# Score products of two heads on the two halves of TensorE's rows, in an fp32 attention and gated feed-forward kernel

## The chip, the core and the metric

The kernel runs on one core of a Trainium2 chip. The metric is the device time of one execution in microseconds, as the median of several runs. The engines are TensorE (PE; its weight loads PEld), VectorE (DVE), ScalarE (ACT), GpSimd (POOL) and the sync engine (SP), which here issues nearly all loads.

## The reference

```python
# q, k, v: (4 batches, 8 heads, 576, 64) fp32; hidden = 32
scores = scale * np.matmul(q, k.transpose(0, 1, 3, 2))
x = (psi_rel / psi_i)[..., None]          # from positions alone
h = np.maximum(x @ w1 + b1, 0.0)
bias = h @ w2                             # one 576 x 576 bias per head
scores = scores + bias.transpose(2, 0, 1)[None, :, :, :]
scores = scores - np.max(scores, axis=-1, keepdims=True)
attn = np.exp(scores)
attn = attn / (np.sum(attn, axis=-1, keepdims=True) + 1e-09)
return np.matmul(attn, v).astype(np.float32)
...
# attn as (2304 tokens, 512), w_in (512, 2048), w_out (2048, 512)
h = x @ w_in
relu6 = np.clip(h + 3.0, 0.0, 6.0)
g = h * relu6 / 6.0
return (g @ w_out).astype(np.float32)
```

The weights w_in and w_out arrive in 64-bit form and are turned into pairs of fp16 numbers (a high and a low part) on the chip.

## The kernel before, in words

**Units and tiles.** Two heads form a pair, four pairs a batch. The 576 query rows are cut in two units: rows 0 to 255 (`u` = 0) and 256 to 575 (`u` = 1). A tile is 128 query rows of one head; a unit 0 has four tiles, a unit 1 five. All 16 units 0 come first. Tile number `n` runs over all of them; of a pair's unit 0 the tiles are row block 0 of head 0, row block 0 of head 1, row block 1 of head 0, row block 1 of head 1 (`ORDER`).

**Two forms of score products.** Batches 0 and 1 of unit 0 (the first 32 tiles) are *direct* (`direct`): score products, transposes of the weights of attention and their product with v are done in fp32. `load_direct` loads q and k of a pair. Head 0 lies on partitions 0 to 63, head 1 on 64 to 127; q is spread to a tile with zeros in the other head's rows (memset on GpSimd, line 378), so that a product over all 128 rows gives one head's scores. All later tiles split q and k into a high and a low part in a packed 32-bit form and take three products a head on 64 rows each, the two heads in turn (line 549); the last row block of a unit 1 takes three products on 128 rows with a zero-filled tile. One fp32 product is two records in the trace, each with its own weight load; one of line 549 is one record.

**A step.** `front(n)` issues, in this order: the score products of tile n+1 if it is direct (`qk_step`), the softmax maximum of tile n on VectorE (line 561, reads the scores and the bias, writes `bt`), for later tiles the score products here instead, the transposes of tile n-2 (line 620, 128 rows, fp32), loads (`aux`), the product with v once a unit is complete (lines 662, 673, then a multiply on VectorE, line 689). `back(n)` issues the exponential on ScalarE (line 572). Between the steps come pieces of other work at fixed rates: the position bias (lines 847 to 864), the preparation of w_in and w_out (lines 244 to 280 and 138) and the feed-forward network (hidden layer line 779 with lines 756 to 769, output layer line 802).

**PSUM.** Until tile 45 there are three score banks (`s_bank`, two PSUM banks each), which score products, transposes, products with v and bias products share in turn, and two `w_bank`s. From tile 45 on there are two and four.

**What sets the order.** A scheduler takes the program order as a priority and sets each engine's order when the program is built, until tile 45; from there TensorE follows the program order. Each engine then runs its list in order and waits where an input or a buffer isn't there. The loads (lines 377, 380, 433, 483 and 489 for the bias, 175 for v, 244 for w) stand in the sync engine's queue in the same way; `behind()` keeps a load behind the last bias load.

Of the kernel before, what the change touches and what calls it, by code (L numbers as in the profile page):

```python
# [10 lines left out]
F32 = mybir.dt.float32  # L11
# [7 lines left out]
S = 576  # L19
# [3 lines left out]
HALF = S // 2  # L23
# [10 lines left out]
def attention_moe_kernel(  # L34
# [15 lines left out]
    nc = tc.nc  # L50
# [11 lines left out]
    qk_p = ctx.enter_context(tc.tile_pool(name="qk", bufs=4))  # L62
# [17 lines left out]
    def s_bank(name):  # L80
        return pools["ps_s"].tile([128, 2, 512], F32, tag="s", name=name)
# [140 lines left out]
    def dq(c):  # L222
        return nc.scalar if c in cfg["act"] else nc.sync
# [3 lines left out]
    def behind(k=-1):  # L227

        return tc.issue_after(bias_loads[k]) if len(bias_loads) > max(k, 0) else nullcontext()
# [138 lines left out]
    qk_t = {}  # L368
    st_t = {}

    def load_direct(b, p):
        t = qk_p.tile([128, 512 + S], F32, tag="hi", name="qk0")
        q, k = t[:, 0:512].rearrange("p (a b) -> p a b", a=2), t[:, 512:512 + S]
        for s in range(2):
            rows = slice(64 * s, 64 * s + 64)
            with behind():
                dq("q").dma_start(out=q[rows, s], in_=qk[b, p][rows, 0:256])
            nc.gpsimd.memset(q[rows, 1 - s], 0.0)
        with behind():
            dq("q").dma_start(out=k, in_=qk[b, p][:, 256:256 + S])  # L380
        qk_t[b, p, 0] = (t, k)

    QW = (256, 320)
    KC0 = (256, 0)
# [128 lines left out]
    s_t = {}  # L513
# [4 lines left out]
    def qk_step(n):  # L518
        b, p, t = tiles[n]
        i, s = ORDER[t]  # L520
        u = int(t >= 4)
        if direct(b, p, t):
            ps = s_bank("s_ps")
            q, k = qk_t[b, p, 0]
            c = 256 * s + 128 * i
            for a in range(2):
                nc.tensor.matmul(  # L527
                    out=ps[:, a, 0:HALF], lhsT=q[:, c:c + 128], rhs=k[:, a * HALF:(a + 1) * HALF]
                )
            s_t[n] = ps  # L530
            return
        if s:
            return
        if i == 4:
            hi, lo, tz = qk_t.pop((b, p, u))
            every = slice(0, 128)
            parts = [(every, tz[:, 0], tz[:, 1])]
        else:
            hi, lo = qk_t[b, p, u][:2]
            c = QC0[u] + 128 * i - 256 * u  # L540
            qs = slice(c, c + 128)
            parts = [(r, hi[r, qs], lo[r, qs]) for r in (slice(0, 64), slice(64, 128))]
        for k in range(len(parts)):
            s_t[n + k] = s_bank("s_ps")
        for k, (q, m) in enumerate(((0, hi), (0, lo), (1, hi))):
            for a in range(2):
                cs = slice(KC0[u] + a * HALF, KC0[u] + (a + 1) * HALF)
                for j, (rows, *w) in enumerate(parts):
                    nc.tensor.matmul(  # L549
                        out=s_t[n + j][:, a, 0:HALF], lhsT=w[q], rhs=m[rows, cs],  # L550
                        start=(k == 0), stop=(k == 2),
                    )
# [47 lines left out]
    def direct(b, p, t):  # L600
        return b < cfg["fb"] and t < 4
# [329 lines left out]
    def front(n):  # L931
        late = at(n + 1) and not direct(*tiles[n + 1])
        if at(n + 1) and not late:
            qk_step(n + 1)
# [6 lines left out]
        if late:  # L941
            qk_step(n + 1)
# [32 lines left out]
    def aux(n):  # L975
        b, p, t = tiles[n]
        k = unit_no[n]
        l = t - UT[int(t >= 4)][0]
        if l == 0 and PAIRS <= k + 2 < len(units):
            b2, p2, u2 = units[k + 2]  # L980
            if direct(b2, p2, 4 * u2):
                load_direct(b2, p2)
            else:
                load_qk(b2, p2, u2)
        if k + 1 < len(units) and not direct(units[k + 1][0], 0, 4 * units[k + 1][2]):
            if l == 1:
                split_qk_a(*units[k + 1])
            if l == 2:
                split_qk_b(*units[k + 1])
            if l == 3:  # L990
                split_qk_c(*units[k + 1])
        if l == 0 and k < 13:
            load_v(*units[k])
        if l == 1 and 13 <= k + 1 < len(units):
            load_v(*units[k + 1])
        if not direct(b, p, t):
            if l == 2:
                split_v_a(*units[k])
            if l == 3:
                split_v_b(*units[k])  # L1000
        if b + 1 < B and t < 4 and p >= 1:
            if b + 1 not in vgen:
                vgen[b + 1] = v_scale(b + 1)
            next(vgen[b + 1], None)
# [26 lines left out]
    for cs in (slice(512, LT), slice(0, 512)):  # L1031
        nc.vector.tensor_scalar(
            out=T[:, cs], in0=T[:, cs], scalar1=w1_sb, scalar2=None, op0=ALU.mult
# [13 lines left out]
    for c, pat in enumerate(pats):  # L1047
        for k in range(4):
            if pat[k]:
                rows = slice(32 * k, 32 * k + 32)  # L1050
# [95 lines left out]
    for g in range(cfg["g0"]):  # L1146
        bias_next()
        if g == 0:
            steps(gen_w, aw, cfg["rwi"])
        if 0 <= g - cfg["gq"] < PAIRS:  # L1150
            load_direct(0, g - cfg["gq"])
        if g >= 1:
            steps(gen_w, aw, cfg["rw0"])
    for n in range(-1, NT + 7):
# [14 lines left out]
        if done is not None and done != (0, 0):  # L1169
            b, u = done  # L1170
# [71 lines left out]
```

## Time and profile before

| | us |
|---|---|
| median of 3 runs | 714.4 |
| lowest and highest | 710.62, 718.45 |
| the profiled execution | 713.93 |
| its span in the trace | 712.1 |

The span is the stretch from the first to the last instruction in the trace; 1.8 us of the profiled execution lie around it. The median and the profiled execution differ by 0.5 us. The profile has one core, with a mean granted TensorE clock of 0.976 of full speed.

### The profile page before, as it was taken

Reading aid. Unit: us, or ns where it says so; the run is one execution under the profiler, and the core shown is the slowest. Engines: PE = TensorE matmul, PEld = TensorE weight load, DVE = VectorE, ACT = ScalarE, POOL = GpSimd, SP = SyncE. Lnnn points to the kernel's source line nnn. Section 1 sums busy time; section 2 is a strip of 40 time slices with the busy share of each in tenths; the row PEclk is TensorE's granted clock in tenths of the full one; section 3 lists DMA queues with packets and bytes.
Section 4 is the critical chain, followed back from the end, with each engine's and each line's share of the span. In section 5 each row is a group of like instructions: output and inputs, shape, how many; then the busy total and the mean of one; then the engine's idle time right before and its main releaser. Section 6 shows DMA issues by size and latency. Waiting matters only on the chain. (4 is left out here: it accounts for less than half of the span.)

```text
span 712.1 us, 15431 instructions
## 1 busy us (share of the span) xinstructions
PE 657.8 (92%) x5538; PEld 471.2 (66%) x5538; DVE 498.2 (70%) x1263; ACT 491.8 (69%) x994; POOL 257.0 (36%) x350
## 2 busy tenths in 40 slices
PE   6667799898889998999998899999999999999998
PEld 2214566676466676788786788767776777777775
DVE  7999788899777697758866877777767776310310
ACT  6996678788676798758866876888568854631530
POOL 3212021346222154236642563465335611420420
PEclk9889999999999999999999999999999999999999
DMA  8987987856695996999999998969995865000000
GB/s 279 337 284 215 312 241 207 252 151 182 173 216 145 240 224 172 226 245 204 224 222 236 193 205 179 218 158 185 187 199 135 171 144 111 2 10 28 2 11 28
DMA packets 178637, 127.35 MB, mean 179 GB/s; under 512 B 139136, under 2 KB 147584, under 8 KB 178560
## 3 DMA queue, kind: packets, MB, share of 16 engines
q1 hardware_dynamic: 168768, 111.03, 67.0%
q10 hardware_dynamic: 9792, 15.34, 6.9%
q8 instruction: 43, 0.70, 0.4%
q14 instruction: 34, 0.28, 0.1%
HBM read 74.43 MB, written 15.34 MB: 126 GB/s over the span
## 5 line engine op out<-in xcount | busy, mean ns | idle before, releaser
L779 PE MATMUL h_ps<-x,wi 128*128 128x256 f16 (+1 forms) x1536 | 198.6, 287 | 8.0 <-DVE t L762 4.5
L802 PE MATMUL o_ps<-g,wo 128*128 128x256 f16 (+1 forms) x1536 | 196.6, 287 | 0.0
L779 PEld LDWEIGHTS <-wi 128*128 128x128 f16 x1536 | 147.1, 98 | 54.1 <-issue 12.3
L802 PEld LDWEIGHTS <-wo 128*128 128x128 f16 x1536 | 147.1, 98 | 47.0 <-issue 9.9
L758 POOL TENSOR_TENSOR g<-t,g 128x256 f16<-128x256 f32 (+1 forms) x128 | 101.9, 806 | 135.3 <-ACT g L756 134.4
L572 ACT ACTIVATE bt<-bt,sm 128x576 f32<-128x576 f32 x144 | 110.6, 768 | 56.1 <-DVE sm L561 55.3
L138 DVE SCALAR_TENSOR_TENSOR hl<-bt,sm,hl 128x576 f16<-128x576 f32 x112 | 98.7, 891 | 23.8 <-POOL hl L115 13.7
L762 DVE SCALAR_TENSOR_TENSOR t<-t,t,h_ps 128x320 f32<-128x320 f32 (+1 forms) x112 | 56.1, 516 | 68.4 <-ACT t L769 67.5
L115 POOL TENSOR_SCALAR hl<-bt,sm 128x576 f16<-128x576 f32 x56 | 48.9, 873 | 109.4 <-DVE sm L584 55.1
L864 PE MATMUL b_ps<-z,w_sb 128*32 128x288 f32 x576 | 68.5, 445 | 18.6 <-ACT z L851 15.5
L756 ACT ACTIVATE g<-t 128x256 f16<-128x256 f32 (+1 forms) x128 | 55.5, 440 | 35.3 <-DVE t L762 34.5
L404 POOL TENSOR_TENSOR qkl<-st,qkh 128x576 fp32r<-128x576 f32 (+2 forms) x48 | 56.1, 1188 | 43.9 <-ACT qkh L397 42.2
L769 ACT ACTIVATE t<-h_ps,t,hr 128x320 f32<-128x320 f32 (+1 forms) x112 | 64.7, 586 | 9.5 <-PE h_ps L779 6.3
L561 DVE CUSTOM_DVE_ANT_0 bt<-s_ps,bt 128x576 f32<-128x576 f32 x80 | 58.9, 751 | 10.3 <-PE s_ps L549 8.3
L864 PEld LDWEIGHTS b_ps<-z,w_sb 128*32 128x32 f32 x576 | 21.2, 113 | 54.1 <-ACT z L851 30.0
L812 ACT ACTIVATE ot<-o_ps,os 128x256 f32<-128x256 f32 (+1 forms) x32 | 15.9, 497 | 55.7 <-PE o_ps L802 54.7
L847 DVE TENSOR_SCALAR z<-T,nbp 128x576 f32<-128x576 f32 x85 | 51.0, 641 | 3.3 <-PE b_ps L864 3.2
L851 ACT ACTIVATE z<-T,bp 128x576 f32<-128x576 f32 x59 | 45.1, 767 | 11.7 <-PE b_ps L864 8.1
L561 DVE CUSTOM_DVE_ANT_0 bt<-s_ps,k 128x576 f32<-128x576 f32 x64 | 46.2, 752 | 6.3 <-PE s_ps L549 5.0
L527 PE MATMUL s_ps<-qk 128*128 128x288 f32 x128 | 41.2, 448 | 9.9 <-DVE sm L561 4.4
L121 ACT ACTIVATE hl<-bt,sm 128x576 f16<-128x576 f32 x56 | 43.1, 769 | 6.8 <-issue 1.5
L580 DVE TENSOR_SCALAR sm<-sm 128x1 f32<-128x1 f32 x112 | 16.8, 150 | 41.7 <-ACT bt L572 41.4
(118 smaller groups left out, 880.7 us busy)
## 6 DMA issues: line engine op xcount, KB each, us to landing
bt<-bias SPq DMA_DIRECT2D x64, 288.0 KB, 5.5
bias<-bo ACTq DMA_DIRECT2D x36, 288.0 KB, 4.8
w<-in_w_in_dram SPq DMA_DIRECT2D x16, 512.0 KB, 5.5
vs<-in_vp_dram SPq DMA_DIRECT2D x24, 320.0 KB, 5.1
st<-in_qk_dram SPq DMA_DIRECT2D x16, 448.0 KB, 4.4
wo<-in_w_out_dram SPq DMA_DIRECT2D x10, 512.0 KB, 7.1
k<-bias SPq DMA_DIRECT2D x32, 144.0 KB, 3.7
bt<-bias SPq DMA_DIRECT2D x32, 144.0 KB, 3.2
```

Of the source, the lines that this page charges most:

```text
L138: nc.vector.scalar_tensor_tensor(out=out, in0=full, scalar=scale, in1=high, op0=ALU.mult, op1=ALU.subtract)
L404: nc.gpsimd.tensor_sub(out=lo[:, c:c + w], in0=t[:, c:c + w], in1=hi[:, c:c + w].bitcast(F32))
L561: nc.vector.tensor_tensor_reduce(out=halves(bt), in0=ps, in1=halves(src), op0=ALU.add, op1=ALU.min, scale=-0.125, scalar=3.0e38, accum_out ...
L572: nc.scalar.activation(out=bt, in_=bt, func=AF.Exp, scale=-1.0, bias=sm[:, 0:1], accum_out=total)
L756: nc.scalar.activation(out=g[:, 0], in_=uu, func=AF.Copy)
L758: e.tensor_sub(out=g[:, 1], in0=uu, in1=g[:, 0])
L762: nc.vector.scalar_tensor_tensor(out=t_t[f], in0=t_t[f], scalar=cols(f)[2], in1=h_t.pop(f)[:, 0:n], op0=ALU.min, op1=ALU.mult,)
L769: nc.scalar.activation(out=t_t[f], in_=h_t[f][:, 0:n], func=AF.Relu, scale=cols(f)[0], bias=cols(f)[1],)
L779: nc.tensor.matmul(out=h_t[f][:, 0:n], lhsT=wi[:, a, c, f * 128:(f + 1) * 128], rhs=x[:, e, c], start=(k == 0), stop=(k == 3 * KC - 1),)
L802: nc.tensor.matmul(out=ops[:, 0:n], lhsT=wo[:, a, f, e * 128:(e + 1) * 128], rhs=g_t[f][:, r], start=(f == 0 and a == 0 and r == 0), stop= ...
L847: nc.vector.tensor_scalar(out=z, in0=src, scalar1=nbp[:, col], scalar2=None, op0=ALU.max)
L864: nc.tensor.matmul(out=pss[a][32 * k:32 * k + 32, 0:HALF], lhsT=w2_sb, rhs=z[:, a * HALF:(a + 1) * HALF],)
```

## The change

`load_direct` loads q and k of a pair with one transfer into one tile and writes no zeros. `qk_step` does nothing for a tile of head 1; for a tile of head 0 it takes two score banks and issues the products of both heads, each on the 64 rows of its head, the heads in turn for each half of the columns. The later lines move up by four (line 549 becomes 545, 620 becomes 616).

```diff
     def load_direct(b, p):
-        t = qk_p.tile([128, 512 + S], F32, tag="hi", name="qk0")
-        q, k = t[:, 0:512].rearrange("p (a b) -> p a b", a=2), t[:, 512:512 + S]
-        for s in range(2):
-            rows = slice(64 * s, 64 * s + 64)
-            with behind():
-                dq("q").dma_start(out=q[rows, s], in_=qk[b, p][rows, 0:256])
-            nc.gpsimd.memset(q[rows, 1 - s], 0.0)
+        t = qk_p.tile([128, 512 + S], F32, tag="hi", name="qk0")[:, 0:256 + S]
         with behind():
-            dq("q").dma_start(out=k, in_=qk[b, p][:, 256:256 + S])
-        qk_t[b, p, 0] = (t, k)
+            dq("q").dma_start(out=t, in_=qk[b, p][:, 0:256 + S])
+        qk_t[b, p, 0] = t
...
+        if s:
+            return
         if direct(b, p, t):
-            ps = s_bank("s_ps")
-            q, k = qk_t[b, p, 0]
-            c = 256 * s + 128 * i
+            m = qk_t[b, p, 0]
+            for k in range(2):
+                s_t[n + k] = s_bank("s_ps")
             for a in range(2):
-                nc.tensor.matmul(
-                    out=ps[:, a, 0:HALF], lhsT=q[:, c:c + 128], rhs=k[:, a * HALF:(a + 1) * HALF]
-                )
-            s_t[n] = ps
-            return
-        if s:
+                cs = slice(256 + a * HALF, 256 + (a + 1) * HALF)
+                for k in range(2):
+                    r = slice(64 * k, 64 * k + 64)
+                    nc.tensor.matmul(
+                        out=s_t[n + k][:, a, 0:HALF], lhsT=m[r, 128 * i:128 * i + 128], rhs=m[r, cs]
+                    )
             return
```

On TensorE, before, at the end of the first batch and the start of the second (`qk_848` is the fifth pair's tile of q and k, `bt` a tile's attention weights; x2 and x5 are instructions in a row):

```order
L620 MATMUL t_ps<-eye_sb,bt 128x128 x5
L527 MATMUL s_ps<-qk_848 128x288 x2
L620 MATMUL t_ps<-eye_sb,bt 128x128 x5
L662 MATMUL pv_ps<-atf,vf 64x256 x10
L673 MATMUL pv_ps<-eye_sb,r_sb 64x128 x4
L527 MATMUL s_ps<-qk_848 128x288 x2
L620 MATMUL t_ps<-eye_sb,bt 128x128 x5
L527 MATMUL s_ps<-qk_848 128x288 x2
```

The same place on TensorE in the changed program (`qk_832` is the fifth pair's tile there):

```order
L616 MATMUL t_ps<-eye_sb,bt 128x128 x10
L658 MATMUL pv_ps<-atf,vf 64x256 x10
L669 MATMUL pv_ps<-eye_sb,r_sb 64x128 x4
L526 MATMUL s_ps<-qk_832 128x288 x4
L616 MATMUL t_ps<-eye_sb,bt 128x128 x10
```

Products and transposes of one tile in turn have become products of two tiles, then transposes of two tiles.

On VectorE, before, around the last tiles of the fourth pair's second row block (`k_776` is a kept bias tile; the ISA rows are the softmax maximum and its read-out):

```order
L561 ISA bt,sm<-s_ps,k_776 128x576
L561 ISA sm 128x1
L138 SCALAR_TENSOR_TENSOR wo<-cu,w2s,wo 128x512
L144 TENSOR_REDUCE m_v_855<-vparts 128x1
L561 ISA bt,sm<-s_ps,k_776 128x576
L561 ISA sm 128x1
L1103 TENSOR_SCALAR x<-x,r_w1c 128x2x256
L147 TENSOR_SCALAR m_v_855<-m_v_855 128x1
L561 ISA bt,sm<-s_ps,bt 128x576
```

The same place on VectorE in the changed program (`k_763` is that bias tile):

```order
L557 ISA bt,sm<-s_ps,k_763 128x576
L557 ISA sm 128x1
L557 ISA bt,sm<-s_ps,k_763 128x576
L557 ISA sm 128x1
L1099 TENSOR_SCALAR x<-x,r_w1c 128x2x256
L273 TENSOR_SCALAR cu,w2top<-cu 128x512
L144 TENSOR_REDUCE m_v_835<-vparts 128x1
L138 SCALAR_TENSOR_TENSOR wo<-cu,w2s,wo 128x512
L557 ISA bt,sm<-s_ps,bt 128x576
```

The softmax maxima of the two heads now stand one behind the other, and the other work stands between the pairs.

## Rows read from the trace of the kernel before

**Rows 1.** The page: busy time of each engine, share of the span, instructions.

```profile
PE 657.8 (92%) x5538; PEld 471.2 (66%) x5538; DVE 498.2 (70%) x1263; ACT 491.8 (69%) x994; POOL 257.0 (36%) x350
```

**Rows 2.** Stretches: length, then each engine's busy time, granted clock, DMA share, GB/s.

```profile
54.00:100.00 46.00, 34.62 (x195) 23.00 (x187) 38.88 (x113) 31.02 (x60) 7.38 (x14) 0.93 0.87 255
100.00:184.00 84.00, 77.98 (x561) 57.49 (x559) 75.22 (x223) 68.00 (x142) 33.63 (x43) 0.96 0.73 207
184.00:230.00 46.00, 41.82 (x370) 26.29 (x369) 35.73 (x98) 32.22 (x57) 11.66 (x14) 0.96 0.72 168
230.00:712.00 482.00, 467.14 (x4178) 352.89 (x4170) 298.80 (x721) 315.72 (x670) 191.45 (x253) 1.00 0.72 154
```

**Rows 3.** Instructions of lines 527, 549: shortest, median, longest ns, first and last start.

```profile
L527 PE MATMUL s_ps<-qk x128: 405/407/849, 54.7 to 157.3; 128*128 128x288 f32 x128
...
L549 PE MATMUL s_ps<-qkh x192: 285/395/607, 158.2 to 592.1; 64*128 64x288 f32 x192
```

**Rows 4.** Stretches, line 527 alone: length, PE busy, PEld busy, clock, DMA.

```profile
54.00:100.00 46.00, 18.87 (x56) 10.55 (x56) 0.93 0.87 255
100.00:160.00 60.00, 22.33 (x72) 12.76 (x72) 0.97 0.75 212
```

**Rows 5.** Waits of VectorE, 54 to 184 us: total us, times, longest.

```profile
DVE vparts L177 <- DMA va<-in_vp_dram: 7.0, 5, 2.0
...
DVE bt L561 <- PE s_ps L527: 1.5, 1, 1.5
```

**Rows 6.** Waits of TensorE's matmuls, 54 to 184 us.

```profile
PE s_ps L527 <- DVE sm L561: 4.4, 3, 2.5
PE s_ps L527 <- DVE xr L689: 4.1, 2, 3.7
```

**Rows 7.** Timeline of TensorE's matmuls from 102.9 us: start, us, what.

```profile
102.93 1.14 PE L527 MATMUL s_ps<-qk 128*128 128x288 f32 x4
103.91 0.71 PE L620 MATMUL t_ps<-eye_sb,bt 128*128 128x128 f32 x5
```

**Rows 8.** Chain of work that ended last: start, us, what.

```profile
473.05 0.79 PE s_ps L549 x6
...
483.49 0.99 PE s_ps L549 x12
```

**Rows 9.** Timeline of TensorE's matmuls from 204.9 us.

```profile
204.92 1.18 PE L864 MATMUL b_ps<-z,w_sb 128*32 128x288 f32 x16
206.03 4.43 PE L802 MATMUL o_ps<-g,wo 128*128 128x256 f16 x39
```

**Rows 10.** Timeline of TensorE's matmuls from 138.4 us.

```profile
138.37 2.78 PE L779 MATMUL h_ps<-x,wi 128*128 128x256 f16 x24
140.99 1.14 PE L527 MATMUL s_ps<-qk 128*128 128x288 f32 x4
```

**Rows 11.** Timeline of GpSimd from 74.9 us; in brackets the idle time before.

```profile
74.92 0.66 POOL L378 MEMSET qk<- 64x256 f32 x2 [9.53 <-PE s_ps L527]
79.70 0.66 POOL L258 TENSOR_SCALAR wo<-wo 128x512 f32<-128x512 f32 x1 [4.12 <-ACT cu L256]
```

**Rows 12.** The sync queue: line 377 (ns as in rows 3), and its timeline.

```profile
L377 SPq DMA_DIRECT2D qk<-in_qk_dram x16: 471/594/656, 6.4 to 119.1; - x16
...
76.33 1.25 SPq L377 DMA_DIRECT2D qk<-in_qk_dram  x2
```

**Rows 13.** Transfers by line: count, KB each, median us from issue to landing.

```profile
st<-in_qk_dram SPq DMA_DIRECT2D x8, 416.0 KB, 6.0
```

**Rows 14.** Timeline of VectorE, 93 to 103 us.

```profile
93.13 0.34 DVE L1103 TENSOR_SCALAR x<-x,r_w1c 128x512 f16<-128x512 f16 x1
...
95.03 0.76 DVE L561 CUSTOM_DVE_ANT_0 bt<-s_ps,bt 128x576 f32<-128x576 f32 x1 [1.50 <-PE s_ps L527]
...
95.72 0.68 DVE L273 TENSOR_SCALAR_CACHE_REDUCE cu<-cu 128x512 f32<-128x512 f32 x1
...
102.95 0.75 DVE L138 SCALAR_TENSOR_TENSOR wo<-cu,w2s,wo 128x512 f16<-128x512 f32 x1
```

## Prediction, made before the changed kernel had run

> **What bounds the kernel now.** I read the page first: TensorE is busy for 92% of the span, VectorE for 70% and ScalarE for 69% [rows 1]. That is an average over very different stages, so the second view is a table by stretches [rows 2]. After 230 us TensorE is busy for 467.1 of 482 us: there the end moves only with TensorE's work, or with the moment at which that stage starts. The work that the change touches lies ahead of it: the 128 matmul records of line 527 run from 54.7 to 157 us [rows 3], 18.87 us of busy time before 100 us and 22.33 us after it [rows 4]; at four records a tile that is 14 tiles and 18 tiles. So the question is how much sooner the first 230 us end. In 54 to 100 us TensorE is busy for 34.6 of 46 us and VectorE for 38.9; in 100 to 184 us it is TensorE 78.0 of 84, VectorE 75.2; in 184 to 230 us TensorE 41.8 of 46, VectorE 35.7 [rows 2]. Neither engine is alone the bound there. The two wait lists for 54 to 184 us say who waits for whom: VectorE's longest wait is for a load (va, 7.0 us in five waits), and for score products it waited once, for 1.5 us [rows 5]; the matmul side's longest waits on line 527 are for VectorE's softmax, 4.4 us, and for its normalising multiply, 4.1 us [rows 6]. So before 100 us TensorE mostly waits for a VectorE that itself waits for data, and after 100 us TensorE is nearly full.
>
> **The products themselves.** A tile of the old form takes 0.98 us: its four records start at 102.93 us and the transposes behind them at 103.91 us [rows 7]. Two tiles are 1.96 us. No fp32 product of which two take the two halves of the rows in turn is in the trace. The nearest rows are those of line 549: a packed pair of heads, 12 matmuls on 64 rows each, took 0.99 us in the chain, and six matmuls on 128 rows took 0.79 us [rows 8]. Six rounds of two therefore ran abreast, and the pair paid 0.20 us more than its six rounds. That fp32 products run abreast too is shown by another row: 16 fp32 records of the bias products, in four column groups, had passed after 1.11 us (204.92 to 206.03 us) [rows 9], where four unpacked ones need 0.98 us. So a pair of the new form is four rounds of 0.245 us plus 0.20 us, 1.18 us, and saves 0.78 us. With 16 pairs that is **12.5 us of TensorE time**; the bounds are 15.7 us (nothing paid for the change of form) and a loss of 3.2 us (no two abreast, 16 times 0.20 us paid).
>
> The 0.20 us is what the row shows for going from 128 rows to 64 and back. The Trainium skill, "TensorEngine Tiling (Array Packing)", section Key Properties, says that changing the tiling mode drains TensorE; it speaks against this change, since every pair stands between transposes on 128 rows. It gives no price: with no drain the sum would be 15.7 us, with the row's 0.20 us it is 12.5 us, and the trace agrees with the rule.
>
> **What of it reaches the end.** Seven pairs run before 100 us: 7 x 0.78 = 5.5 us at full clock. TensorE has 11.4 idle us there and waits mostly for VectorE, whose waits for va are not TensorE's doing. I take 1.5 us of the 5.5; bounds 0 and 5.5. Nine pairs run after 100 us: 7.0 us, in a stage with 6.0 idle us of TensorE. Here the products are ahead of the hidden-layer matmuls (line 779) that fill the gaps, 0.109 us each (24 of them from 138.37 to 140.99 us) [rows 10]. The order of the changed program shows where they go: 120 of the 192 of the first unit stand ahead of the first line-549 product, 90 before; 30 x 0.109 = 3.3 us of work pulled ahead. VectorE limits it: 8.8 idle us in the stage, some of it waits that stay. I take 5.5 of the 7.0 us; bounds 2 and 7. The sum is **7.0 us**. What is late next is VectorE: at 84 - 5.5 us the stage holds 75.2 us of its work, 96%. The steady stage after 230 us holds the same work as before, so I carry the 7.0 us to the end unchanged.
>
> **The rest of the diff.** The 16 memsets (line 378) go. They cost GpSimd 0.3 us each; the worst of them stood 9.53 us waiting for line 527 to free its buffer, but the operation behind it then waited another 4.12 us for ScalarE, so nothing was lost by it [rows 11]: zero. If that cover were gone, it would be worth at most those 9.53 us to the preparation of w_out, none to the products. The three loads of a pair become one: 16 issues fewer of 0.594 us each, 9.5 us of the sync queue's time [rows 12], which is free where that queue waits for buffers anyway. The new load has the size of an existing one, which landed in 6.0 us [rows 13]. The fifth pair's load was issued at 76.3 us and its first product ran at 102.9 us [rows 7, 12], so 20 us cover it: zero. On the queue, the loads of pairs one to three now stand ahead of the w_in chunks that were between them, and the first four w_out chunks stand ahead of two bias loads instead of behind them. These have waits of their own (for VectorE and ScalarE), and behind them queue bias loads that a softmax needs; I price it at 0, with 2 us either way, the longest single wait for a load in [rows 5].
>
> **Rivals.** (1) *Order of the score banks: slower.* The pair takes two of three score banks at once, and the products of the next pair can't start before the softmax of the second head has read its bank, where one tile could run ahead before. If VectorE has nothing else queued, it stands idle for a pair's products each time: 1.18 us and a hop, about 1.3 us; the one such wait in the trace is 1.50 us [rows 14]. 16 x 1.3 = 21 us, less the 12.5 saved: 713.9 + 21 - 12.5 = **722 us**. It decides once fewer than 1.3 us of other work stand on VectorE between two pairs. The changed order speaks against it: between the two softmaxes of a pair and the next ones it has a scaling of x, a step of w_out's preparation and a low part, 0.34 + 0.68 + 0.75 = 1.8 us [rows 14], and often more. The Trainium skill, same page, Gotcha 1, warns that row tiling increases PSUM pressure; with three banks this is the place where that would show. (2) *VectorE is the bound, the gain is hidden:* the idle time of TensorE only grows, and 54 to 230 us keep their length but for the one 1.5 us wait: **713 us**. For it: VectorE's 90% in 100 to 184 us; against it: TensorE's 93% there. (3) *More than forecast:* all 12.5 us arrive, **701 us**, if the va loads are also no longer waited for; in the changed order more work stands on VectorE ahead of the first va reductions. (4) *The two heads don't run abreast in fp32:* 713.9 + 3.2 = **717 us**. Against it speak [rows 8, 9].
>
> **How the numbers follow.** The profiled execution took 713.93 us, 0.5 us under the median of 714.4, so the sum stands against either: 713.9 - 7.0 = 706.9, **707.0 us**. Chances: forecast (703 to 710.5) 0.46, rival 2 (710.5 to 715) 0.24, rival 3 (698 to 703) 0.15, rival 4 0.06, rival 1 0.09. One per cent is 7.1 us, about what a measurement can tell from no change, so the line is at 707.3 us. Faster by more: rival 3 and two thirds of the forecast, 0.46. Slower by more: rival 1, 0.09. Within 1%: 0.45. The range of 8 in 10 leaves out rival 1 and the fast end of rival 3, and keeps rival 4: **699 to 717 us**.
>
> **What would show it.** Right: the line of the score products has 128 records on 64 rows, two starting within a few ns, and about 20 us busy instead of 41.2; TensorE's busy time falls by 10 to 15 us; the first line-549 product comes some 5 to 8 us sooner than 158.2 us [rows 3]. Wrong: VectorE waits for s_ps many times (rival 1); the same start of the first line-549 product with more idle TensorE (rival 2); records of a pair 0.245 us apart one after another (rival 4). If the front stage ends sooner but the time stays, the gain was given back after 184 us, where I carried it over without a price.

## The result: 722.3 us, 1.1% slower, and the profile after

The changed kernel took 722.33 us (median of 5 runs, 718.9 to 726.39), the kernel before 714.4 us (710.62 to 718.45). The ratio is 1.011, with a 95% interval of 1.0078 to 1.0143. The profiled execution of the changed kernel is the slowest of its five, 726.39 us, so its trace shows some 4 us more than the median does. In the changed kernel the packed fp32 score products are line 526, those of the next stage line 545, the softmax is line 557, transposes are line 616 and the copy that empties their bank is line 619.

The page's busy row of the changed kernel answers to [rows 1]:

```profile
PE 662.7 (91%) x5538; PEld 469.2 (65%) x5538; DVE 497.2 (69%) x1263; ACT 492.6 (68%) x994; POOL 252.3 (35%) x334
```

TensorE was to lose 10 to 15 us of busy time; it gained 4.9. The stretches of the changed kernel answer to [rows 2] (length, busy time of each engine, granted clock, DMA share, GB/s):

```profile
54.00:100.00 46.00, 32.88 (x153) 20.77 (x152) 39.08 (x109) 29.54 (x58) 5.84 (x10) 0.70 0.87 260
100.00:184.00 84.00, 74.50 (x523) 51.53 (x524) 69.39 (x203) 62.94 (x129) 26.31 (x35) 0.90 0.63 174
184.00:230.00 46.00, 41.46 (x349) 26.36 (x348) 36.88 (x105) 34.26 (x65) 12.67 (x16) 0.96 0.84 196
230.00:724.00 494.00, 479.93 (x4258) 359.64 (x4256) 302.69 (x728) 320.06 (x678) 194.93 (x257) 0.99 0.74 153
```

The column to read is the granted clock: 0.70 instead of 0.93 in 54 to 100 us, 0.90 instead of 0.96 in 100 to 184 us. From 54 us on, TensorE is busy for 628.8 us of 670 (before: 621.6 of 658) and idle for 41.2 (before: 36.4). The score products fell from 41.2 us [rows 4] to 33.3 us (the page's group of line 526). So all other work of TensorE, unchanged in what it computes, takes 7.2 + 7.9 = 15.1 us longer, and idle time adds 4.8: 15.1 + 4.8 - 7.9 = 12.0 us, the difference between the two traces from 54 us on. The clock column, times TensorE's busy share in each stretch, gives an estimate of what the lower clock costs: 46 x 0.23 x 0.72 = 7.6 us in 54 to 100 us, 84 x 0.06 x 0.89 = 4.5 us in 100 to 184 us, and, since 0.99 stands against 1.00 over 494 us, up to some 5 us after 230 us. Together that is about the 15.1 us: the longer work is the lower clock, and half of it falls in the first batch's stage.

The lower clock is no accident of the profiled execution. The mean granted clock of each whole execution is on record: 0.953 to 0.959 in the five of the changed kernel, 0.962 to 0.988 in the 71 of the kernel before that ran beside the experiments.

The score products of the changed kernel answer to [rows 3] (shortest, median, longest ns; first and last start):

```profile
L526 PE MATMUL s_ps<-qk x128: 402/403/846, 53.6 to 170.0; 64*128 64x288 f32 x128
...
L545 PE MATMUL s_ps<-qkh x192: 285/394/606, 174.2 to 604.3; 64*128 64x288 f32 x192
```

There are 128 records on 64 rows, as forecast, but the first product of the next stage starts at 174.2 us instead of 158.2 us. Some 2.6 us of these 16 are only a change of order: 120 records of the hidden layer run ahead of it where 96 did, at 0.109 us each [rows 10]. Where the rest went is seen in stretches of 10 us, TensorE alone (length, busy time, clock, DMA share, GB/s), first before, then after:

```profile
62.00:72.00 10.00, 6.38 (x26) 0.83 0.72 195
72.00:82.00 10.00, 7.35 (x43) 1.00 1.05 349
82.00:92.00 10.00, 6.28 (x45) 0.99 1.05 277
```

```profile
62.00:72.00 10.00, 5.67 (x17) 0.50 0.70 204
72.00:82.00 10.00, 7.35 (x21) 0.50 1.04 349
82.00:92.00 10.00, 10.00 (x57) 0.64 1.03 306
92.00:102.00 10.00, 7.26 (x54) 1.00 0.62 169
```

0.50 is the lower of the two levels, 1.2 GHz. TensorE's timeline of the changed kernel shows what that costs (start, us, what, records, in brackets the idle time before):

```profile
73.74 2.29 PE L526 MATMUL s_ps<-qk 64*128 64x288 f32 x4
...
79.16 2.29 PE L526 MATMUL s_ps<-qk 64*128 64x288 f32 x4 [2.62 <-ACT atf L619]
81.38 2.39 PE L616 MATMUL t_ps<-eye_sb,bt 128*128 128x128 f32 x10
...
84.64 2.30 PE L526 MATMUL s_ps<-qk 64*128 64x288 f32 x8
86.87 2.40 PE L616 MATMUL t_ps<-eye_sb,bt 128*128 128x128 f32 x10
...
92.24 1.25 PE L526 MATMUL s_ps<-qk 64*128 64x288 f32 x8
93.42 0.77 PE L616 MATMUL t_ps<-eye_sb,bt 128*128 128x128 f32 x5
...
105.00 1.24 PE L526 MATMUL s_ps<-qk 64*128 64x288 f32 x8
```

The packing works: at 84.64 us eight records take as long as four do. At 2.4 GHz (105.00 us) a pair takes 1.24 us, where one old tile took 1.14 us [rows 7]; counted from its start to the start of the next work, a pair takes 1.18 us (92.24 to 93.42 us) and an old tile 0.98 us. But at 1.2 GHz a pair takes 2.23 us in the same count (84.64 to 86.87 us), more than two old tiles at full clock (1.96 us). Three of the 16 pairs are split in the plan: each head's four records stand apart, as at 73.74 and 79.16 us, where the second four wait 2.62 us for ScalarE's copy (line 619). Four records alone take as long as eight, so these gain nothing. Ten transposes take 2.39 us where before five took 0.71 [rows 7].

The waits of VectorE in 54 to 184 us answer to [rows 5] (total us, times, longest), with one place of its timeline:

```profile
DVE vparts L177 <- DMA va<-in_vp_dram: 4.3, 3, 3.1
DVE bt L557 <- PE s_ps L526: 3.6, 4, 1.5
```

```profile
144.75 0.82 DVE L177 TENSOR_REDUCE vparts<-va 128x1 f32<-128x640 f32 x1 [3.10 <-DMA va<-in_vp_dram]
...
146.66 0.82 DVE L177 TENSOR_REDUCE vparts<-va 128x1 f32<-128x640 f32 x1 [1.01 <-DMA va<-in_vp_dram]
```

VectorE waits for score products a little more often (3.6 us instead of 1.5). It waits for v less in all than before (4.3 us instead of 7.0), and nearly all of that in one place, at 142 to 147 us.

### The profile page after: what moved, and what is told of

The parts are those of the page before. It is cut to its first block, busy times and chain, and to the rows that moved or that the text cites. A ratio compares the mean times of both kernels' runs of the same rounds, so it can differ in the third digit from the quotient of the medians.

```text
span 724.6 us, 15381 instructions
## 1 busy us (share of the span) xinstructions
PE 662.7 (91%) x5538; PEld 469.2 (65%) x5538; DVE 497.2 (69%) x1263; ACT 492.6 (68%) x994; POOL 252.3 (35%) x334
## 5 line engine op out<-in xcount | busy, mean ns | idle before, releaser
L775 PE MATMUL h_ps<-x,wi 128*128 128x256 f16 (+1 forms) x1536 | 201.7, 290 | 9.5 <-DVE t L758 4.6
L798 PE MATMUL o_ps<-g,wo 128*128 128x256 f16 (+1 forms) x1536 | 198.7, 287 | 0.3 <-DVE x L138 0.3
L775 PEld LDWEIGHTS <-wi 128*128 128x128 f16 x1536 | 148.9, 99 | 58.4 <-issue 16.8
L860 PE MATMUL b_ps<-z,w_sb 128*32 128x288 f32 x576 | 65.1, 427 | 20.0 <-ACT z L847 17.9
L752 ACT ACTIVATE g<-t 128x256 f16<-128x256 f32 (+1 forms) x128 | 55.3, 439 | 33.3 <-DVE t L758 32.7
L765 ACT ACTIVATE t<-h_ps,t,hr 128x320 f32<-128x320 f32 (+1 forms) x112 | 64.8, 586 | 12.5 <-PE h_ps L775 9.0
L843 DVE TENSOR_SCALAR z<-T,nbp 128x576 f32<-128x576 f32 x85 | 49.1, 621 | 5.0 <-PE b_ps L860 4.9
L526 PE MATMUL s_ps<-qk 64*128 64x288 f32 x128 | 33.3, 511 | 9.2 <-DVE sm L557 5.9
```

What stands on the lines that cost most here:

```text
L752: nc.scalar.activation(out=g[:, 0], in_=uu, func=AF.Copy)
L765: nc.scalar.activation(out=t_t[f], in_=h_t[f][:, 0:n], func=AF.Relu, scale=cols(f)[0], bias=cols(f)[1],)
L775: nc.tensor.matmul(out=h_t[f][:, 0:n], lhsT=wi[:, a, c, f * 128:(f + 1) * 128], rhs=x[:, e, c], start=(k == 0), stop=(k == 3 * KC - 1),)
L798: nc.tensor.matmul(out=ops[:, 0:n], lhsT=wo[:, a, f, e * 128:(e + 1) * 128], rhs=g_t[f][:, r], start=(f == 0 and a == 0 and r == 0), stop= ...
L860: nc.tensor.matmul(out=pss[a][32 * k:32 * k + 32, 0:HALF], lhsT=w2_sb, rhs=z[:, a * HALF:(a + 1) * HALF],)
```

## The experiments

Four theories were tested. **A:** TensorE spends much longer at 1.2 GHz in the direct stage (at first: because it has less to do there; later, as **A2**: because the score products of the first batch use 64 rows). **B:** a pair takes two of the three score banks at once. **C:** loads now stand in another order, and those of v come late. **D:** every edit makes the build plan the order of all engines anew, and it is the order of the kernel before that is lost. All times are medians; the ratio is to runs of the kernel before in the same session. By D every experiment also changes the order, so its time alone can't tell an effect of a few us from that of the new order.

**1. Pair order, 128 rows.** The kernel before, but with both heads' products written together, as in the change, into two banks:

```diff
+        if s:
+            return
...
-            ps = s_bank("s_ps")
...
+            for h in range(2):
+                s_t[n + h] = s_bank("s_ps")
             for a in range(2):
...
+                for h in range(2):
+                    c = 256 * h + 128 * i
...
```

> Before with the order of the change alone: zeros, three loads a pair and products on all 128 rows stay, but the products of both heads are issued together and take two score banks at once. Theory A (the changed kernel is slow because TensorE, with less to do in 54 to 90 us, falls to the lower clock for long): TensorE's work is that of before, so about 714 us (712 to 716) and less than 20 us at the lower clock between 54 and 184 us, where the changed kernel has 44 us. Theory B (two of three score banks taken at once make TensorE and VectorE wait for each other, whatever the products cost): 720 to 726 us, with softmax waits like those of the changed kernel. Theory C (the new order of loads in the sync queue): about 714 us.

Measured: 727.1 us, ratio 1.0141 (1.01 to 1.0182), first product of the next stage (the kernel before's line 549) at 167.6 us. Up to 184 us the clock hardly falls; it does in the next stretch:

```profile
54.00:100.00 46.00, 35.75 (x189) 22.20 (x183) 38.61 (x106) 31.82 (x61) 7.35 (x14) 0.89 0.88 254
100.00:184.00 84.00, 74.40 (x527) 54.04 (x524) 69.39 (x206) 62.59 (x131) 27.96 (x37) 0.96 0.66 186
184.00:230.00 46.00, 38.97 (x306) 24.05 (x305) 37.86 (x106) 32.99 (x61) 14.32 (x16) 0.89 0.90 194
```

So more time is lost than by the change itself, without packing and without the long stretch at 1.2 GHz. The order written for a pair, with the two banks that it takes and the plan that comes of it, is enough.

**2. One tile at a time, 64 rows.** The changed kernel, with each head's product at its own turn and in its own bank:

```diff
+            ps = s_bank("s_ps")
...
-            for k in range(2):
-                s_t[n + k] = s_bank("s_ps")
+            r = slice(64 * s, 64 * s + 64)
...
```

> One load a pair and no zeros as in the change, each head on its own 64 rows, but one tile at a time as before, so nothing runs abreast and one bank is taken at a time. Theory A: TensorE's busy time is that of before plus the change of form, so 713 to 717 us. Theory B: 714 us. Theory C: 720 us or more, since the order of loads is that of the change.

Measured: 728.6 us, 1.0174 (1.014 to 1.0207). With one bank a tile the loss is no smaller, so B isn't needed for it. TensorE's work is that of before, nothing runs abreast, and A's first reason (less to do) forecast 713 to 717 us; the clock is at 0.50 with TensorE all but fully busy:

```profile
72.00:82.00 10.00, 9.39 (x28) 0.50 1.04 319
82.00:92.00 10.00, 10.00 (x29) 0.50 1.04 322
```

**3. The packed products twice.** `for a in (0, 1, 0, 1)` instead of `for a in range(2)`; the second pass computes the same values again.

```diff
-            for a in range(2):
+            for a in (0, 1, 0, 1):
```

> The changed kernel with each pair of score products computed twice into the same bank (the first result is overwritten), so that TensorE's work on line 526 is about that of before (some 39 us at full clock) with the banks, loads and order of the change. Theory A: back to 713 to 717 us and less than 25 us at the lower clock between 54 and 184 us. Theory B: as slow as the change or slower, 722 to 730 us. Theory C: 722 us or more.

Measured: 744.11 us, 1.0425 (1.0385 to 1.0466). The profiled execution took 752.18 us, 8 us over the median. More work on 64 rows does not bring the clock back, and A's first reason, by which the time was to be 713 to 717 us, falls:

```profile
62.00:72.00 10.00, 8.18 (x21) 0.51 0.68 194
72.00:82.00 10.00, 6.71 (x16) 0.50 0.92 331
82.00:92.00 10.00, 7.73 (x27) 0.50 0.59 199
```

**4. Packed inside one tile.** The two column halves of one head's tile run on the two row halves, q is loaded twice, six loads a pair, one bank a tile:

```diff
+            m, c = qk_t[b, p, 0], (256 + HALF) * s
             for a in range(2):
+                r = slice(64 * a, 64 * a + 64)
                 nc.tensor.matmul(
...
+                    out=ps[:, a, 0:HALF], lhsT=m[r, c + 128 * i:c + 128 * i + 128],
+                    rhs=m[r, c + 256:c + 256 + HALF],
                 )
```

> Packing without pairs: a head's q is loaded to both halves of the rows, the first half of its k columns to the upper rows and the second to the lower, so that the two column halves of ONE tile run abreast and one bank is taken at a time, in the order of before (no zeros; six loads a pair, q twice). Line 529's busy time about 25 us. Theory A: as slow as the change, 718 to 726 us, with over 30 us at the lower clock between 54 and 184 us. Theory B: 706 to 712 us, since the banks are free of pairs and 8 to 12 us of TensorE work are gone. Theory C has no say here: the queue order is a third one.

Measured: 727.1 us, 1.0174 (1.0131 to 1.0218); clock in 54 to 100 us 0.74. Packing without the pair, in one bank a tile and with six loads instead of one, loses no less.

**5. Only the rows.** The kernel before with its zeros, loads and banks; the products read the 64 rows that aren't zero:

```diff
-                    out=ps[:, a, 0:HALF], lhsT=q[:, c:c + 128], rhs=k[:, a * HALF:(a + 1) * HALF]
+                    out=ps[:, a, 0:HALF], lhsT=q[64 * s:64 * s + 64, c:c + 128], rhs=k[64 * s:64 * s + 64, a * HALF:(a + 1) * HALF]
```

> The kernel before with its zeros, its three loads of a pair and its two score banks; only the 128 products of the direct tiles read 64 of the 128 rows, those whose other half is zeros in the kernel before. The times planned for these products differ a little, so some transfers and small products change places as well. Theory A (a product on 64 rows lets the granted TensorE clock fall for long in this stage): a stretch at 1.2 GHz of 15 us or more that begins between 60 and 80 us, tiles some 8 us late by tile 10, a time of 722 to 729 us. Theory D (every version is re-planned as a whole, and what is lost is the order of the kernel before): no long stretch at 1.2 GHz, but tiles 26 and later some 5 to 12 us late, 719 to 727 us. If both are wrong, 713 to 716 us, as the kernel before.

Measured: 725.73 us, 1.0124 (1.0083 to 1.0165); first line-549 product at 168.9 us. Stretches of TensorE, and its group of score products:

```profile
62.00:72.00 10.00, 6.19 (x18) 0.57 0.66 192
72.00:82.00 10.00, 9.50 (x28) 0.50 1.04 321
82.00:92.00 10.00, 10.00 (x30) 0.50 1.04 331
```

```profile
L527 PE MATMUL s_ps<-qk 64*128 64x288 f32 x128 | 46.3, 488 | 5.3 <-DVE sm L561 3.6 <-ACT atf L623 1.3 <-DVE xr L689 0.4
```

Half the rows, the same number of records, and the products take 46.3 us instead of 41.2. This is the strongest single support for A2; its plan differs from that of the kernel before in places, so it doesn't stand alone.

**6. k loaded first.** The kernel before, with the load of k issued ahead of q and its zeros; no work is changed:

```diff
+        with behind():
+            dq("q").dma_start(out=k, in_=qk[b, p][:, 256:256 + S])
         for s in range(2):
...
-        with behind():
-            dq("q").dma_start(out=k, in_=qk[b, p][:, 256:256 + S])
```

> The kernel before with the load of k issued ahead of the two loads of q and their zeros instead of behind them; products, banks, bytes and instruction counts are those of the kernel before. As a result some transfers and small products are planned in another order. Theory D (the order is what was lost): 719 to 727 us, with the tiles from 26 on some 5 to 12 us late as in the other variants, though nothing was made slower. Theory A (the clock under 64-row products): no effect, 713 to 716 us, and no stretch at 1.2 GHz over 7 us between 54 and 100 us.

Measured: 725.71 us, 1.0161 (1.0115 to 1.0207): more than the change itself costs, from an edit that slows nothing. Its first line-549 product starts at 156.4 us, sooner than before; the time goes afterwards:

```profile
54.00:100.00 46.00, 35.67 (x198) 23.89 (x199) 38.39 (x112) 31.71 (x63) 9.38 (x14) 0.93 0.94 267
...
184.00:230.00 46.00, 40.19 (x290) 23.12 (x289) 31.90 (x89) 28.39 (x50) 8.38 (x11) 0.81 0.62 145
```

In 184 to 230 us the clock is 0.81 and 290 matmul records ran where 370 did [rows 2]. D holds for this kernel, in another place than where the change loses.

**7. Work on 128 rows added.** The changed kernel with six fp16 products ahead of each direct tile's transposes, into their bank, where the transposes overwrite them:

```diff
+            eye16 = eye_sb.bitcast(F16)
+            for _ in range(6):
+                nc.tensor.matmul(out=tp[:, 0:256], lhsT=eye16[:, 0:128], rhs=eye16[:, 0:256])
```

> The changed kernel with six fp16 products of 128 rows and 256 columns put ahead of the five transposes of each direct tile, into the transposes' own bank, where they are overwritten: work that only adds activity on all 128 rows. By the 0.131 us that an fp16 product of 128x256 takes, it is 0.8 us of TensorE a tile, 25 us over 32 tiles. Theory A (the clock falls since 64-row products leave the array half idle): the long stretch at 1.2 GHz from 62 us is gone or under 7 us, the tiles 6 to 13 come 4 to 8 us earlier than in the changed kernel, and the time is at or below it in spite of the added work, 712 to 722 us. Theory D: the clock may return but the time does not, 722 to 735 us.

Measured: 730.58 us, 1.021 (1.0178 to 1.0242). Stretches of TensorE, and the added products' group:

```profile
62.00:72.00 10.00, 7.55 (x28) 0.50 0.77 226
72.00:82.00 10.00, 10.00 (x63) 0.87 1.03 345
82.00:92.00 10.00, 7.31 (x62) 0.99 1.05 303
92.00:102.00 10.00, 7.66 (x33) 0.50 0.46 133
```

```profile
L616 PE MATMUL t_ps<-eye_sb 128*128 128x256 f16 x192 | 30.3, 301 | 8.2 <-DVE xr L688 3.8 <-DVE sm L557 2.3 <-ACT atf L622 1.4
```

The clock is back in 72 to 82 us (0.87), where with twice the 64-row work (run 3) it stayed at 0.50; 30.3 us of added records cost 8.3 us over the changed kernel. But it falls again after 92 us, and the time is not below the changed kernel's: that the rows matter to the clock (A2) is supported, the forecast of the time (712 to 722 us) missed.

**8. v loads on the scalar engine's queue.** In the changed kernel, for the second and later batches:

```diff
-                dq("v").dma_start(out=t, in_=vp[b, p])
+                (nc.scalar if b else nc.sync).dma_start(out=t, in_=vp[b, p])
```

> The changed kernel with the v loads of the second and later batches issued from the scalar engine's queue instead of the sync engine's, where they stand behind bias loads that wait for transposes. Theory C (the second step of the loss, at tile 26, comes from these loads): VectorE's wait for them at 144 to 147 us (4.3 us in the changed kernel) goes below 1 us, and tiles from 26 on are 3 to 5 us earlier, 716 to 720 us. If the loads were only late because everything ahead of them was, or another wait takes their place: 721 to 725 us, as the changed kernel.

Measured: 722.96 us, 1.0126 (1.0085 to 1.0168). In 136 to 160 us VectorE waits no longer for v; its longest wait there is another:

```profile
DVE t L758 <- ACT t L765: 2.8, 1, 2.8
```

The wait went and the time stayed. C, which forecast 716 to 720 us, isn't borne out as the cause; a gain of a few us that another order took away is not excluded.

**9. The same edit on the kernel before.**

> The kernel before with the v loads of the second and later batches on the scalar engine's queue: the same edit as in the run of the changed kernel with that edit (722.96 us), so that the two are a pair planned anew alike. If products on 64 rows are what costs time (theory A), the kernel before keeps its lead in the pair: 713 to 717 us. If the lead of the kernel before is its order, which any edit spoils (theory D): 721 to 729 us, so that the packed products stand level with the padded ones or ahead of them once both have been planned anew.

Measured: 718.49 us, 1.0046 (1.0015 to 1.0078), between the two forecasts: the edit costs the kernel before 0.5%, and its lead over the changed kernel with the same edit (run 8, ratio 1.0126) is 0.8% instead of 1.1%.

**10. Weights' loads one step further back.** The changed kernel with `'wb': 4` instead of 3, a step that changes no instruction's place in the kernel before:

```diff
-CFG = {... 'wb': 3, ...}
+CFG = {... 'wb': 4, ...}
```

> The changed kernel with the number that sets how far the loads of the weights stand behind others in the plan at 4 instead of 3; in the kernel before the same step changes the place of no instruction, in the changed kernel it puts bias and v loads ahead of the loads of w_out again, as they stand in the kernel before. Theory C (the late v and bias loads make the loss): VectorE's wait for v at tile 26 goes, tiles from 26 on some 4 us earlier, 714 to 719 us. Theory D (another order, not a better one in particular): within 716 to 728 us. Theory A: no effect on the stretch at 1.2 GHz from 62 us, 720 to 724 us.

Measured: 723.22 us, 1.0122 (1.0082 to 1.0161); clock in 54 to 100 us 0.71. The first bias and v loads of this stage stand ahead of those of w_out again, as in the kernel before, but in 136 to 160 us VectorE waits for v nearly as long as in the changed kernel:

```profile
DVE vparts L177 <- DMA va<-in_vp_dram: 3.5, 2, 2.1
```

So this run doesn't test C: the wait that was to go stayed, and so did the time.

**11 and 12. Bias tiles at most five tiles ahead**, `'la': 5` instead of 6, in the kernel before (11) and the changed one (12):

```diff
-CFG = {... 'la': 6, ...}
+CFG = {... 'la': 5, ...}
```

> The kernel before with the bias tiles loaded at most five tiles ahead instead of six: a second edit made alike on both kernels, which changes the order and no work. Theory D: 719 to 729 us, although the products are the 128-row ones. Theory A: 713 to 718 us.

> The changed kernel with the same edit, bias tiles at most five tiles ahead. Theory D: within 3 us of the kernel before with that edit, or below it, since the packed products take 8 us of TensorE less. Theory A: some 8 us above it, as the unedited pair is, with a stretch at 1.2 GHz of 15 us or more between 54 and 100 us.

Measured: before 725.64 us, 1.017 (1.0124 to 1.0216); changed 716.66 us, 1.0037 (1.0004 to 1.007). In this pair the packed kernel is 9 us the faster one. It still has its stretch at 1.2 GHz (clock 0.68 in 54 to 100 us, first line-545 product at 172.6 us).

**13 to 16. Half of the change, each half in two plans.** `packed(b)` chooses between the old and the new form by batch; 13 and 15 pack the second batch's 16 direct tiles, 14 and 16 the first batch's; 15 and 16 have `'la': 5`.

```diff
+    def packed(b):
+        return b == 1
```

> Half of the change: the 16 direct tiles of the first batch (54 to about 105 us) as in the kernel before, with zeros, three loads and 128-row products; those of the second batch packed on 64 rows with one load. Theory A2 (64-row score products let the clock fall in the first batch's stage, where TensorE has little else between them): no stretch at 1.2 GHz over 7 us between 54 and 100 us, tiles 6 to 15 within 4 us of the kernel before. The half that is packed then saves up to 6 us of TensorE, so that by the clock alone 711 to 716 us; with another order of the plan on top, 714 to 724 us. Theory D alone (only the order counts): a stretch of 15 us or more can come here as well, 716 to 728 us.

> The other half: the direct tiles of the first batch packed on 64 rows, those of the second as in the kernel before. Theory A2: the stretch at 1.2 GHz of 15 us or more that begins between 60 and 70 us is here, as in every kernel whose first batch has 64-row products, and tiles 8 to 15 are 5 to 10 us late; 720 to 730 us. Theory D alone: no more likely here than in the other half.

> The first half (second batch packed) with bias tiles loaded at most five tiles ahead: a second plan of the same work, for whether the stretch at 1.2 GHz goes with the rows or with the plan. Theory A2: none over 7 us between 54 and 100 us. The time by the spread that plans showed so far (714 to 727 us with 128-row products, 717 to 729 us with 64-row products): 712 to 725 us.

> The other half (first batch packed) with bias tiles at most five tiles ahead. Theory A2: the stretch of 15 us or more from 60 to 70 us is here again, tiles 8 to 15 are 5 to 10 us late. The time by the spread of plans: 716 to 728 us.

Measured: 13: 721.24 us, 1.0084 (1.0054 to 1.0114); 14: 718.07, 1.0039 (1.0014 to 1.0064); 15: 723.64, 1.013 (1.009 to 1.017); 16: 714.13, 1.0004 (0.9976 to 1.0031). TensorE in the same stretches of 10 us, kernels 13, 14, 15 and 16 in turn:

```profile
62.00:72.00 10.00, 6.76 (x23) 0.74 0.70 193
72.00:82.00 10.00, 7.95 (x41) 0.91 1.03 337
82.00:92.00 10.00, 6.94 (x50) 0.94 1.06 261
```

```profile
62.00:72.00 10.00, 6.73 (x24) 0.50 0.77 213
72.00:82.00 10.00, 5.42 (x15) 0.50 1.03 332
82.00:92.00 10.00, 10.00 (x41) 0.52 0.92 290
```

```profile
62.00:72.00 10.00, 6.59 (x21) 0.69 0.69 184
72.00:82.00 10.00, 6.79 (x32) 0.84 1.02 337
82.00:92.00 10.00, 9.21 (x35) 0.50 1.04 256
```

```profile
62.00:72.00 10.00, 5.79 (x20) 0.56 0.78 216
72.00:82.00 10.00, 7.79 (x28) 0.67 1.04 351
82.00:92.00 10.00, 9.60 (x59) 0.75 1.05 289
```

The long stretch is in kernel 14 and not in 13, as A2 said. With `'la': 5` A2's forecasts of the clock missed: kernel 15 has ten microseconds and more of it with 128-row products, and kernel 16 a broken one. The rows make it likely, they are not the only condition. And the time doesn't follow it: in both plans the half with the first batch packed is the faster one (14 ahead of 13, 16 ahead of 15), and 14 and 16 came in below A2's 720 to 730 us and the 716 to 728 us forecast for them.

**All runs in one view.** Mean granted clock in 54 to 100 us against the form of the first batch's products:

| first batch's products | kernels | clock 54 to 100 us | time, us |
|---|---|---|---|
| 128 rows | before, 1, 6, 9, 11, 13, 15 | 0.93 0.89 0.93 0.89 0.93 0.89 0.76 | 714.4 727.1 725.7 718.5 725.6 721.2 723.6 |
| 64 rows | after, 2, 4, 5, 8, 10, 12, 14, 16 | 0.70 0.63 0.74 0.67 0.72 0.71 0.68 0.67 0.78 | 722.3 728.6 727.1 725.7 723.0 723.2 716.7 718.1 714.1 |
| 64 rows and added work | 3, 7 | 0.67 0.76 | 744.1 730.6 |

The clock column parts the two forms almost without overlap; the time column doesn't. The mean clock of whole executions, a median for each kernel, points the same way with less distance: 0.950 to 0.965 for the nine kernels of the second row, 0.964 to 0.978 for those of the first. Kernels with the same products and only another order (before, 6, 9 and 11) lie between 714.4 and 725.7 us; fully packed ones (after, 8, 10, 12) between 716.7 and 723.2 us.

## Why the prediction was wrong

**The products: right in kind, the term too large.** They run abreast, and the price of a pair was right: 1.18 us was forecast and 1.18 us measured at 2.4 GHz, in the count from start to next start that the forecast used. So rival 4 falls. The sum of 12.5 us of TensorE time measured 7.9 (41.2 to 33.3 us busy), because five of the 16 pairs ran at 1.2 GHz in whole or in part and three were split. The sign "about 20 us busy instead of 41.2" never followed from that sum: it sets 16 pairs at full clock against a measured time that holds slow stretches, and by the count of 0.98 us the old tiles at full clock are 31.4 us.

**What of it reaches the end: this step failed.** "Seven pairs run before 100 us: 7 x 0.78 = 5.5 us at full clock" took the clock of the trace of before as given. With 64-row products in the first batch it is not: 0.63 to 0.78 in 54 to 100 us in all eleven such kernels, against 0.89 to 0.93 in six of seven with 128 rows. In the profiled execution that stage's clock alone costs an estimated 7.6 us, as much as the products save, where the sum had no term at all. The clock falls here in the kernel before too (0.83 in 62 to 72 us), but there it is back at 1.00 in the next 10 us; in the changed kernel it stays down for some 27 us (10 + 10 + 7.2, by 0.50, 0.50 and 0.64). That the 64-row products keep it down is what the halves (13 against 14), run 5 and what brings it back (7 against 3) show, within limits: each of these kernels also has a plan of its own, and in runs 15 and 16 the clock is nearly the same (0.76 and 0.78) with 128 rows and with 64. The further 4.5 us in 100 to 184 us are no mark of the 64 rows: of the other kernels with them, run 10 has 0.91 there and seven (2, 4, 5, 8, 12, 14, 16) have 0.94 to 0.98, where the changed one has 0.90 and the kernel before 0.96.

**The rest of the diff at 0, with 2 us either way: this step failed too.** A move of loads that changes no work (run 6) cost 11.2 us against the kernel before in its session, and one number of the plan 9.3 us (run 11). The price of moving instructions is not bounded by the longest single wait in the trace, because the order up to tile 45 is planned anew; and in the traces it comes as idle time and lower clock in later stages (0.81 in 184 to 230 us in run 6). The range of 2 us was built from the waits of one plan. What the new order costs in the changed kernel itself is not measured apart.

**Carried to the end unchanged: right for idle time.** After 230 us TensorE is idle for 14.1 us in the changed kernel (494.0 - 479.93) and was for 14.9 us before, so what is late at 230 us is not made up by waiting less. The clock of 0.99 instead of 1.00 adds up to some 5 us in this trace; the profiled execution is 4 us over the median, and no run shows whether that part is typical.

**Rival 1** named 722 us, the time that was measured, but that is luck, since its mechanism isn't what happened: VectorE waited for score products four times, 3.6 us in all, not 16 times, and with one bank a tile (run 2) nothing came back. Rivals 2 and 3 fall with the time.

**Which of the two makes the 1.1%?** Both terms are as large as the result, and the runs don't part them for this one pair. The change is slower by 1.1% as it stands, by 0.8% with v's loads on another queue (8 and 9), and faster by 9.0 us, 1.3%, with bias tiles five ahead (11 and 12). What is shown is that in the changed kernel's trace the clock of the first batch's stage takes back about what the packed products save, and that the sign of the whole hangs on the plan it is put into. What decides which plan is good, and why kernel 15 slowed down with 128 rows, stays open. No version beat the kernel before; kernel 16 equals it.

## What to carry to other kernels

Before pricing a smaller or narrower product at full clock, ask whether the clock of that stage will hold, and price the case in which all of the stage's TensorE work runs at 1.2 GHz. Where a build plans the order anew after every edit, measure first what an edit that changes no work costs, on both kernels: here 2 to 11 us on the kernel before (runs 9, 11 and 6), where 7 us were forecast, so a single pair of times says little about the edit itself. Read a stage by its granted clock and by the matmul records that ran in it. One mark on the way, as the start of the next stage, misleads where the order changes: in run 6 it came 2 us sooner than in the kernel before and the time was 11 us longer, in run 12 it came 14 us later (172.6 us) and the time was 716.7 us, against 716.4 us.

## What the runs showed of the hardware

TensorE can be busy for all of a stretch and stay at 1.2 GHz: in run 5 it was busy for 9.50 and 10.00 of two times 10 us at 0.50, with fp32 products on 64 rows between transposes on 128; with 128-row products the kernel before ran there at 1.00 and 0.99 while busy for only 7.35 and 6.28 us. Added 64-row products left the clock at 0.50 (run 3); added fp16 products on 128 rows had it at 0.87 in 72 to 82 us and 0.99 in 82 to 92 us (run 7). fp32 products of two heads on the two halves of the rows do run abreast: eight records in 2.30 us where four took 2.29 us at 1.2 GHz.
